# Group normalisation with 4 MB tiles and one group per partition, in place of 2 MB tiles and a cross-partition step, with a rewritten loop

## The chip, the cores and the metric

The kernel runs on one core of a Trainium2 chip. The metric is the device time of one execution in microseconds (us), median over several executions. The span in a profile runs from the first to the last instruction of the profiled execution and is here 1 to 2 us shorter than the metric. All runs quoted were classed as fast.

The engines are called by these names in the profile: PE is the matmul engine, PEld its weight loads, DVE is VectorE, ACT is ScalarE, POOL is GpSimd, and SPq is the queue from which the loads and stores are issued. L156 means line 156 of the kernel of that profile, so one function has different line numbers before and after. SBUF is the memory on the chip in which the tiles lie, in 128 partitions; PSUM is the memory into which the matmuls write.

## The reference

```python
# x: 128 samples x 1024 channels x 32 x 16, bf16; 32 groups of 32 channels
xr = x.reshape(B, G, C // G, H, W)
mu = xr.mean(axis=(2, 3, 4), keepdims=True)
var = ((xr - mu) ** 2).mean(axis=(2, 3, 4), keepdims=True)
xn = (xr - mu) / jnp.sqrt(var + 1e-5)
return xn.reshape(B, C, H, W) * g[None, :, None, None] + b[None, :, None, None]
```

A group has 32 x 512 = 16384 elements. The whole input is 134.2 MB, and the output is as large, so 268.4 MB have to be moved.

## The kernel before

A tile holds two samples in 128 partitions: 16 channels (16 KB) per partition, two partitions to a group, 2 MB in all, 64 tiles, eleven buffers. A matmul with a matrix of ones for partitions of the same group sums a tile over both partitions; VectorE reduces the resulting 512 columns to the mean. ScalarE takes the squares, and one quarter of the sum for the mean. A second small matmul joins the squares of the two partitions. Then come root, reciprocal, scale and bias, 16 scalings on VectorE (one per channel), and the store.

```python
# M: sums of a tile on PE (12 of 16 chunks; ScalarE's M1 sums the other 4)
nc.tensor.matmul(out=ps[:], lhsT=ind_b[:], rhs=xt[:, k*MMN:(k+1)*MMN], ...)
# R: columns -> -mean, on VectorE
nc.vector.tensor_scalar(out=jd[:], in0=st["ps"][:], ..., accum_out=negmean[:])
# Q: squares on ScalarE          # Gm: across partitions, on PE     # T: root on ScalarE
# A: reciprocal, scl, bia, then 16 scalings in place, on VectorE    # S: store
...
for s in range(-1, NT + 2):          # (bounds checks cut)
    M1(s + 1); M(s + 1)
    Gm(s - 1)
    A(s - 2)
    R(s + 1)
    Q(s)
    T(s - 1)
    S(s - 2); L(s - 2 + PREFETCH)
```

The order in which instructions are emitted is kept on each engine, for all that go through the kernel's helper `chain`. The scalings of step `s` belong to tile `s - 2`, the squares to tile `s`, the mean to tile `s + 1`. So the squares of a tile use a mean whose reduction was given to VectorE one step earlier, and ScalarE does not have to wait for it.

## Time and profile before

| | before |
|---|---|
| time, median | 639.52 us (639.23 to 639.78, 4 runs) |
| ScalarE busy | 590.7 us, 93% of the span |
| VectorE busy | 421.0 us, 66% |
| DMA | 430 GB/s in mid run, main queue 98.7% of the span |

Slices of the page of the kernel before: the span is cut into 40 equal pieces; a digit is the busy share in tenths, 9 meaning 90% or more.

```profile
ACT  1999999999999999999999999999999999999920
DMA  8999999999999999999999999999999999999993
GB/s 357 427 427 426 428 425 429 434 428 423 434 429 429 430 431 432 430 431 430 432 429 431 432 431 431 428 431 433 431 429 430 432 432 430 429 432 431 430 423 163
```

ScalarE and DMA are both full from the second slice to nearly the last. The digits can't tell them apart; the busy times in stretches of 100 us can (busy us and instructions of each engine, then clock, DMA share and GB/s):

```profile
200.00:300.00 100.00, 57.33 (x151) 21.84 (x154) 71.61 (x229) 99.64 (x53) 0.00 (x0) 0.68 1.01 431
500.00:600.00 100.00, 49.32 (x138) 20.42 (x140) 68.87 (x220) 97.11 (x51) 0.00 (x0) 0.68 1.01 430
```

In the order PE, PEld, DVE, ACT, POOL: ScalarE is busy 99.64 of 100 us early on and 97.11 late. It is ahead at first on prefetched tiles and slows in the last stretch, when loads come at DMA's pace: between 500 and 600 us it waits for loads for 2.6 us and PE for 48.9, between 200 and 300 us neither does. One pass of the loop in the timeline (start us, duration, engine, line, instruction; in brackets how long the engine was idle before and who released it):

```profile
301.19 0.24 ACT L221 ACTIVATE rstd<-ps_1567,eps_t 128x1 f32<-128x1 f32 x1
301.33 1.90 ACT L137 ACTIVATE ja<-xt 128x2048 bf16<-128x2048 bf16 x1
301.46 0.16 DVE L232 RECIPROCAL rstd<-rstd 128x1 f32<-128x1 f32 x1 [2.62 <-ACT rstd L221]
...
302.21 5.26 DVE L255 TENSOR_SCALAR xt<-xt,scl,bia 128x512 bf16<-128x512 bf16 x16
...
303.36 7.12 ACT L189 ACTIVATE ja<-xt,negmean 128x8192 bf16<-128x8192 bf16 x1
...
307.38 0.75 DVE L171 TENSOR_SCALAR_CACHE_REDUCE jd<-ps,ps_1616 128x512 bf16<-128x512 f32 x1
...
310.48 0.24 ACT L221 ACTIVATE rstd<-ps_1616,eps_t 128x1 f32<-128x1 f32 x1
```

The root repeats after 310.48 - 301.19 = 9.29 us, and the bracket on ScalarE's rows is absent: ScalarE does not wait in this pass. VectorE does its 16 scalings beside it and then waits 2.62 us, at no cost. A 2 MB tile in and out takes DMA 4.19 MB / 430 GB/s = 9.75 us, so the two limits are 5% apart, and DMA, the slower, sets the time in the long run.

### The profile page before, as it was taken

To read this page: it belongs to the slowest core of one execution; us is meant where nothing else is said; L and a number is where in the kernel's file an instruction comes from. 1 tells how busy PE (TensorE), PEld (TensorE's weight loads), DVE (VectorE), ACT (ScalarE), POOL (GpSimd) and SP (SyncE) were. 2 spreads that over 40 slices of the span, in tenths; PEclk is the share of its full clock that TensorE was granted. 3 is DMA by queue.
4 is the path that set the end of the run, shared out by engine and by line. 5 is a ranking of instruction groups with operands and counts; after the bars stand their busy time and mean duration, and the time that the engine had idled before them with its cause. 6 is when DMAs were issued, how large, how long until landed. Compare 5 with 4: busy or idle time off the path is not lost.

```text
span 637.8 us, 3899 instructions
## 1 busy us (share of the span) xinstructions
PE 326.3 (51%) x887; PEld 127.1 (20%) x904; DVE 421.0 (66%) x1349; ACT 590.7 (93%) x318; POOL 1.6 (0%) x6
## 2 busy tenths in 40 slices
PE   4654564556456555645654664464553654635300
PEld 1221122122112212211221222121221221212100
DVE  0086677668667766866776686677667667767680
ACT  1999999999999999999999999999999999999920
POOL 1000000000000000000000000000000000000000
PEclk9767767776776676666667667766766667666655
DMA  8999999999999999999999999999999999999993
GB/s 357 427 427 426 428 425 429 434 428 423 434 429 429 430 431 432 430 431 430 432 429 431 432 431 431 428 431 433 431 429 430 432 432 430 429 432 431 430 423 163
DMA packets 18774, 268.69 MB, mean 421 GB/s; under 512 B 2368, under 2 KB 2368, under 8 KB 2368
## 3 DMA queue, kind: packets, MB, share of 16 engines
q1 hardware_dynamic: 18752, 268.45, 98.7%
q8 instruction: 7, 0.11, 0.1%
q14 instruction: 15, 0.12, 0.0%
HBM read 134.23 MB, written 134.22 MB: 421 GB/s over the span
## 4 chain that ended last, share of the span: by engine, by line
ACT 53%; DMA 23%; issue 17%; DVE 2%; PE 1%; SPq 0%; DVEq 0%; ACTq 0%
ACT ja L189 38%; DMA out_dram<-xt 18%; ACT ja L137 14%; DMA xt<-in_x_dram 5%; DVE xt L255 2%; ACT rstd L221 1%; PE ps L154 1%; SPq L121 0%; DVE jd L171 0%; DVE bia L243 0%; DVE scl L237 0%; DVEq L330 0%; DVE rstd L232 0%; ACTq L137 0%
## 5 line engine op out<-in xcount | busy, mean ns | idle before, releaser
L189 ACT ACTIVATE ja<-xt,negmean 128x8192 bf16<-128x8192 bf16 x64 | 455.8, 7122 | 15.2 <-DVE jd L171 13.2
L154 PE MATMUL ps<-xt,ind_b 128*128 128x512 bf16 x759 | 301.9, 576 | 80.3 <-DMA xt<-in_x_dram 73.1
L255 DVE TENSOR_SCALAR xt<-xt,scl,bia 128x512 bf16<-128x512 bf16 x1024 | 336.6, 408 | 2.6 <-DVE bia L243 0.2
L154 PEld LDWEIGHTS <-ind_b 128*128 128x128 bf16 x776 | 108.6, 146 | 244.8 <-issue 162.4
L232 DVE RECIPROCAL rstd<-rstd 128x1 f32<-128x1 f32 x64 | 10.5, 164 | 169.1 <-ACT rstd L221 169.1
L137 ACT ACTIVATE ja<-xt 128x2048 bf16<-128x2048 bf16 x62 | 117.7, 1898 | 2.6 <-DMA xt<-in_x_dram 2.6
L243 DVE SCALAR_TENSOR_TENSOR bia<-scl,negmean,bet 128x16 f32<-128x16 f32 x64 | 15.0, 235 | 2.3
L237 DVE TENSOR_SCALAR scl<-gam,rstd 128x16 f32<-128x16 f32 x64 | 15.0, 234 | 2.2
L189 ACT ACTIVATION_READ_ACCUMULATOR ja<-xt,negmean 128x1 f32 x64 | 11.9, 186 | 0.0
L137 ACT ACTIVATION_READ_ACCUMULATOR ja<-xt 128x1 f32 x62 | 11.7, 189 | 0.0
L171 DVE TENSOR_SCALAR_CACHE_REDUCE jd<-ps 128x512 bf16<-128x512 f32 x2 | 1.4, 692 | 7.9 <-PE ps L154 7.9
L171 DVE TENSOR_SCALAR_CACHE_REDUCE jd<-ps,ps_170 128x512 bf16<-128x512 f32 x1 | 0.8, 755 | 6.6 <-PE ps_170 L206 6.6
L284 DVE CAST gam<-gam_b 128x16 f32<-128x16 bf16 x1 | 0.2, 174 | 6.4 <-DMA gam_b<-in_g_dram 6.4
L206 PE MATMUL ps_3186<-carry,ind_f 128*128 128x1 f32 x2 | 0.6, 362 | 6.7 <-ACT ja L189 6.7
L206 PE MATMUL ps_2155<-carry,ind_f 128*128 128x2 f32 x2 | 0.6, 362 | 4.8 <-ACT ja L137 4.8
L206 PE MATMUL ps_930<-carry,ind_f 128*128 128x2 f32 x2 | 0.6, 364 | 4.8 <-ACT ja L137 4.8
L206 PE MATMUL ps_1812<-carry,ind_f 128*128 128x2 f32 x2 | 0.6, 364 | 4.7 <-ACT ja L137 4.7
L206 PE MATMUL ps_587<-carry,ind_f 128*128 128x2 f32 x2 | 0.6, 364 | 4.7 <-ACT ja L137 4.7
L206 PE MATMUL ps_1469<-carry,ind_f 128*128 128x2 f32 x2 | 0.6, 362 | 4.6 <-ACT ja L137 4.6
L206 PE MATMUL ps_244<-carry,ind_f 128*128 128x2 f32 x2 | 0.6, 364 | 4.6 <-ACT ja L137 4.6
L206 PE MATMUL ps_1126<-carry,ind_f 128*128 128x2 f32 x2 | 0.6, 364 | 4.6 <-ACT ja L137 4.6
L206 PE MATMUL ps_2008<-carry,ind_f 128*128 128x2 f32 x2 | 0.6, 362 | 4.6 <-ACT ja L137 4.6
(319 smaller groups left out, 126.9 us busy)
## 6 DMA issues: line engine op xcount, KB each, us to landing
xt<-in_x_dram SPq DMA_DIRECT2D x64, 2048.0 KB, 24.2
out_dram<-xt SPq DMA_DIRECT2D x64, 2048.0 KB, 28.7
gam_b<-in_g_dram SPq DMA_DIRECT2D x2, 2.0 KB, 7.1
bet_b<-in_b_dram SPq DMA_DIRECT2D x2, 2.0 KB, 6.7
```

Of the source, the lines that this page charges most:

```text
L137: nc.scalar.activation(out=ja[:, 0 : na * MMN], in_=xt[:, (NMM - na) * MMN :], func=ACT.Identity, scale=-inv_n, accum_out=carry[:, 1:2],),
L154: nc.tensor.matmul(out=ps[:], lhsT=ind_b[:], rhs=xt[:, k * MMN : (k + 1) * MMN], start=(k == 0), stop=(k == npe - 1),),
L171: nc.vector.tensor_scalar(out=jd[:], in0=st["ps"][:], scalar1=-inv_n, scalar2=seed, op0=ALU.mult, op1=ALU.add, accum_out=negmean[:],),
L189: nc.scalar.activation(out=ja[:], in_=st["xt"][:], func=ACT.Square, bias=st["negmean"][:], scale=1.0, accum_out=carry[:, 0:1],),
L206: nc.tensor.matmul(out=ps2[:, 0:ncol], lhsT=ind_f[:], rhs=st["carry"][:, 0:ncol], start=True, stop=True,),
L221: nc.scalar.activation(out=rstd[:], in_=st["ps2"][:, 0:1], func=ACT.Sqrt, bias=eps_t[:], scale=inv_n),
L232: chain("dve", nc.vector.reciprocal(out=rstd[:], in_=rstd[:]))
L237: nc.vector.tensor_scalar(out=scl[:], in0=gam[:], scalar1=rstd[:], scalar2=None, op0=ALU.mult),
L243: nc.vector.scalar_tensor_tensor(out=bia[:], in0=scl[:], scalar=negmean[:], in1=bet[:], op0=ALU.mult, op1=ALU.add,),
L255: nc.vector.tensor_scalar(out=xt[:, k * HW : (k + 1) * HW], in0=xt[:, k * HW : (k + 1) * HW], scalar1=scl[:, k : k + 1], scalar2=bia[:, k ...
L284: nc.vector.tensor_copy(out=gam[:], in_=gam_b[:])
```

## The change

The intent: a tile of four samples with one whole group (32 channels, 32 KB) in each partition. Nothing has to be joined across partitions any more; the matmul matrix becomes the identity, ScalarE drops its share of the mean, and DMA rows are twice as long. The kernel keeps six such tiles in SBUF. The loop is rewritten, too. Core of the diff:

```diff
-NSAMP = 2
-XBUFS = 11
-PREFETCH = 9
-ACT_CHUNKS = 4
+XBUFS = 6
+UPFRONT = 6
+AHEAD = 5
+SQ_FREE = 4096
+A_HEAD = 12
...
-    x_v = x.rearrange("(t n) (cb k) h w -> t (n cb) (k h w)", n=NS, cb=CB)
+    x_v = x.rearrange("(t n) (g k) h w -> t (n g) (k h w)", n=NS, g=G)
...          # M: 32 matmuls with lhsT=eye[:]; Q: four squares of 4096 each
+    def V(i):   # variance: sum of 4 on VectorE, root on ScalarE,
+                # reciprocal, scl, bia on VectorE
...
-    for s in range(-1, NT + 2):
-        ...     # M1 M(s+1), Gm(s-1), A(s-2), R(s+1), Q(s), T(s-1), S(s-2), L
+    M(0)
+    R(0)
+    for i in range(NT):
+        Q(i)
+        V(i)
+        if i + 1 < NT:
+            M(i + 1)
+        A(i, 0, A_HEAD)
+        if i + 1 < NT:
+            R(i + 1)
+        A(i, A_HEAD, KC)
+        S(i)
+        j = i + AHEAD
+        if UPFRONT <= j < NT:
+            L(j)
```

The loads of gamma and beta also move from the queue of the tile loads to ScalarE's queue, in eight pieces instead of four.

More of the change, by code (lines that the diff above doesn't have):

```diff
@@ L37 @@
     HW = H * W
-    NS = NSAMP
-    assert B0 % NS == 0 and P % NS == 0
+    assert P % G == 0 and C % G == 0
+    NS = P // G
+    assert B0 % NS == 0
     NT = B0 // NS
-    CB = P // NS
-    assert C % CB == 0
-    KC = C // CB
+    KC = C // G
     F = KC * HW
-    cpg = C // G
-    assert cpg % KC == 0
-    PPG = cpg // KC
-    assert CB % PPG == 0
-    NELEM = cpg * HW
-    inv_n = 1.0 / float(NELEM)
+    inv_n = 1.0 / float(F)
     MMN = MM_FREE
-    assert F % MMN == 0
     NMM = F // MMN
-    assert 0 <= ACT_CHUNKS < NMM
-    x_v = x.rearrange("(t n) (cb k) h w -> t (n cb) (k h w)", n=NS, cb=CB)
-    o_v = out.rearrange("(t n) (cb k) h w -> t (n cb) (k h w)", n=NS, cb=CB)
-    g_v = g.rearrange("(cb k) -> cb k", cb=CB)
-    b_v = b.rearrange("(cb k) -> cb k", cb=CB)
+    NSQ = F // SQ_FREE
+    assert F % MMN == 0 and F % SQ_FREE == 0
+    x_v = x.rearrange("(t n) (g k) h w -> t (n g) (k h w)", n=NS, g=G)
+    o_v = out.rearrange("(t n) (g k) h w -> t (n g) (k h w)", n=NS, g=G)
+    g_v = g.rearrange("(g k) -> g k", g=G)
+    b_v = b.rearrange("(g k) -> g k", g=G)
     consts = ctx.enter_context(tc.tile_pool(name="consts", bufs=1))
@@ L63 @@
     jpool = ctx.enter_context(tc.tile_pool(name="jpool", bufs=1))
-    spool = ctx.enter_context(tc.tile_pool(name="spool", bufs=6))
+    spool = ctx.enter_context(tc.tile_pool(name="spool", bufs=4))
     pspool = ctx.enter_context(
         tc.tile_pool(name="pspool", bufs=3, space=bass.MemoryType.PSUM)
-    )
-    ps2pool = ctx.enter_context(
-        tc.tile_pool(name="ps2pool", bufs=3, space=bass.MemoryType.PSUM)
     )
@@ L82, in chain, with L @@
         return inst
-    ones_f = consts.tile([P, P], F32)
-    nc.vector.memset(ones_f[:], 1.0)
-    ind_f = consts.tile([P, P], F32)
-    nc.gpsimd.affine_select(
-        out=ind_f[:].rearrange("p (a c) -> p a c", c=PPG),
-        in_=ones_f[:].rearrange("p (a c) -> p a c", c=PPG),
-        pattern=[[-PPG, P // PPG], [0, PPG]],
-        compare_op=ALU.is_ge,
-        fill=0.0,
-        base=0,
-        channel_multiplier=1,
-    )
-    nc.gpsimd.affine_select(
-        out=ind_f[:].rearrange("p (a c) -> p a c", c=PPG),
-        in_=ind_f[:].rearrange("p (a c) -> p a c", c=PPG),
-        pattern=[[PPG, P // PPG], [0, PPG]],
-        compare_op=ALU.is_ge,
-        fill=0.0,
-        base=PPG - 1,
-        channel_multiplier=-1,
-    )
-    ind_b = consts.tile([P, P], BF16)
-    nc.vector.tensor_copy(out=ind_b[:], in_=ind_f[:])
+    state = {}
+    def L(i):
+        xt = xpool.tile([P, F], BF16, name="xt")
+        chain("sp", nc.sync.dma_start(out=xt[:], in_=x_v[i]))
+        state[i] = {"xt": xt}
+    for i in range(min(UPFRONT, NT)):
+        L(i)
     eps_t = consts.tile([P, 1], F32)
@@ L114 @@
     bet_b = consts.tile([P, KC], BF16)
-    state = {}
-    def L(i):
-        st = state.setdefault(i, {})
-        xt = xpool.tile([P, F], BF16, name="xt")
-        chain("sp", nc.sync.dma_start(out=xt[:], in_=x_v[i]))
-        st["xt"] = xt
-    def act_part(i):
-        return ACT_CHUNKS if i >= 2 else 0
-    def M1(i):
-        na = act_part(i)
-        if not na:
-            return
-        st = state[i]
-        xt = st["xt"]
-        carry = state[i - 2]["carry"]
-        ja = jpool.tile([P, F], BF16, name="ja")
-        chain(
-            "act",
-            nc.scalar.activation(
-                out=ja[:, 0 : na * MMN],
-                in_=xt[:, (NMM - na) * MMN :],
-                func=ACT.Identity,
-                scale=-inv_n,
-                accum_out=carry[:, 1:2],
-            ),
-        )
+    for n in range(NS):
+        chain("act", nc.scalar.dma_start(out=gam_b[n * G : (n + 1) * G, :], in_=g_v))
+        chain("act", nc.scalar.dma_start(out=bet_b[n * G : (n + 1) * G, :], in_=b_v))
+    ones_b = consts.tile([P, P], BF16)
+    nc.vector.memset(ones_b[:], 1.0)
+    eye = consts.tile([P, P], BF16)
+    nc.gpsimd.affine_select(
+        out=eye[:],
+        in_=ones_b[:],
+        pattern=[[-1, P]],
+        compare_op=ALU.is_equal,
+        fill=0.0,
+        base=0,
+        channel_multiplier=1,
+    )
+    gam = consts.tile([P, KC], F32)
+    bet = consts.tile([P, KC], F32)
+    nc.vector.tensor_copy(out=gam[:], in_=gam_b[:])
+    nc.vector.tensor_copy(out=bet[:], in_=bet_b[:])
     def M(i):
         st = state[i]
-        xt = st["xt"]
-        npe = NMM - act_part(i)
         ps = pspool.tile([P, MMN], F32, name="ps")
-        for k in range(npe):
+        for k in range(NMM):
             chain(
@@ L155, in M @@
                     out=ps[:],
-                    lhsT=ind_b[:],
-                    rhs=xt[:, k * MMN : (k + 1) * MMN],
+                    lhsT=eye[:],
+                    rhs=st["xt"][:, k * MMN : (k + 1) * MMN],
                     start=(k == 0),
-                    stop=(k == npe - 1),
+                    stop=(k == NMM - 1),
                 ),
@@ L167, in R @@
         jd = jpool.tile([P, MMN], BF16, name="jd")
-        seed = state[i - 2]["ps2"][:, 1:2] if act_part(i) else None
         chain(
@@ L174, in R @@
                 scalar1=-inv_n,
-                scalar2=seed,
+                scalar2=None,
                 op0=ALU.mult,
@@ L184, in Q @@
         st = state[i]
-        carry = spool.tile([P, 2], F32, name="carry")
-        ja = jpool.tile([P, F], BF16, name="ja")
-        chain(
-            "act",
-            nc.scalar.activation(
-                out=ja[:],
-                in_=st["xt"][:],
-                func=ACT.Square,
-                bias=st["negmean"][:],
-                scale=1.0,
-                accum_out=carry[:, 0:1],
-            ),
-        )
-        st["carry"] = carry
-    def Gm(i):
-        st = state[i]
-        ncol = 2 if (i + 2 < NT and act_part(i + 2)) else 1
-        ps2 = ps2pool.tile([P, 2], F32, name="ps2")
-        chain(
-            "pe",
-            nc.tensor.matmul(
-                out=ps2[:, 0:ncol],
-                lhsT=ind_f[:],
-                rhs=st["carry"][:, 0:ncol],
-                start=True,
-                stop=True,
-            ),
-        )
-        st["ps2"] = ps2
-    def T(i):
-        st = state[i]
+        sq = spool.tile([P, NSQ], F32, name="sq")
+        for k in range(NSQ):
+            ja = jpool.tile([P, SQ_FREE], BF16, name="ja")
+            chain(
+                "act",
+                nc.scalar.activation(
+                    out=ja[:],
+                    in_=st["xt"][:, k * SQ_FREE : (k + 1) * SQ_FREE],
+                    func=ACT.Square,
+                    bias=st["negmean"][:],
+                    scale=1.0,
+                    accum_out=sq[:, k : k + 1],
+                ),
+            )
+        st["sq"] = sq
+    def V(i):
+        st = state[i]
+        var = spool.tile([P, 1], F32, name="var")
+        jv = spool.tile([P, NSQ], F32, name="jv")
+        chain(
+            "dve",
+            nc.vector.tensor_scalar(
+                out=jv[:],
+                in0=st["sq"][:],
+                scalar1=inv_n,
+                scalar2=None,
+                op0=ALU.mult,
+                op1=ALU.add,
+                accum_out=var[:],
+            ),
+        )
         rstd = spool.tile([P, 1], F32, name="rstd")
@@ L221, in T @@
             nc.scalar.activation(
-                out=rstd[:], in_=st["ps2"][:, 0:1], func=ACT.Sqrt, bias=eps_t[:], scale=inv_n
+                out=rstd[:], in_=var[:], func=ACT.Sqrt, bias=eps_t[:], scale=1.0
             ),
         )
-        st["rstd"] = rstd
-    def A(i):
-        st = state[i]
-        rstd = st["rstd"]
-        negmean = st["negmean"]
-        xt = st["xt"]
         chain("dve", nc.vector.reciprocal(out=rstd[:], in_=rstd[:]))
@@ L245, in A @@
                 in0=scl[:],
-                scalar=negmean[:],
+                scalar=st["negmean"][:],
                 in1=bet[:],
@@ L251, in A @@
         )
-        for k in range(KC):
+        st["scl"], st["bia"] = scl, bia
+    def A(i, lo, hi):
+        st = state[i]
+        xt = st["xt"]
+        for k in range(lo, hi):
             chain(
@@ L257, in A @@
                     in0=xt[:, k * HW : (k + 1) * HW],
-                    scalar1=scl[:, k : k + 1],
-                    scalar2=bia[:, k : k + 1],
+                    scalar1=st["scl"][:, k : k + 1],
+                    scalar2=st["bia"][:, k : k + 1],
                     op0=ALU.mult,
@@ L265, in S @@
     def S(i):
-        st = state[i]
-        chain("sp", nc.sync.dma_start(out=o_v[i], in_=st["xt"][:]))
-        state.pop(i - 3, None)
-    for i in range(min(PREFETCH, NT)):
-        L(i)
-        if i == 0:
-            for n in range(NS):
-                chain(
-                    "sp",
-                    nc.sync.dma_start(out=gam_b[n * CB : (n + 1) * CB, :], in_=g_v),
-                )
-                chain(
-                    "sp",
-                    nc.sync.dma_start(out=bet_b[n * CB : (n + 1) * CB, :], in_=b_v),
-                )
-    gam = consts.tile([P, KC], F32)
-    bet = consts.tile([P, KC], F32)
-    nc.vector.tensor_copy(out=gam[:], in_=gam_b[:])
-    nc.vector.tensor_copy(out=bet[:], in_=bet_b[:])
-    for s in range(-1, NT + 2):
-        if 0 <= s + 1 < NT:
-            M1(s + 1)
-            M(s + 1)
-        if 0 <= s - 1 < NT:
-            Gm(s - 1)
-        if 0 <= s - 2 < NT:
-            A(s - 2)
-        if 0 <= s + 1 < NT:
-            R(s + 1)
-        if 0 <= s < NT:
-            Q(s)
-        if 0 <= s - 1 < NT:
-            T(s - 1)
-        if 0 <= s - 2 < NT:
-            S(s - 2)
-            if s - 2 + PREFETCH < NT:
-                L(s - 2 + PREFETCH)
+        chain("sp", nc.sync.dma_start(out=o_v[i], in_=state[i]["xt"][:]))
+        state.pop(i)
+    M(0)
[13 more added lines that the diff above has]
+            L(j)
 _INS = ['x', 'g', 'b']
```

## The prediction

> **What bounds the kernel now.** Two limits lie almost on each other. The slice rows show DMA at 9 tenths in nearly every slice and about 430 GB/s; one 2 MB tile in and out is 4.19 MB, so 9.75 us at that rate. The timeline shows ScalarE nearly as tight: its squares repeat every 9.29 us (7.12 us square, 1.90 us partial mean, their accumulator reads), and the stretches view shows it 99.6% busy from 100 to 500 us. The chain of waits is DMA from 450 us on. The software pipeline is two tiles deep, so no engine waits for the statistics of its own tile.
>
> **What changes.** Per 4 MB tile (32 of them):
> - DMA: the same bytes, 8.39 MB, 19.5 us at 430 GB/s. The queue is 98.7% busy with 16 KB rows already, so longer rows can save little.
> - PE: 32 identity matmuls, 0.43 us apart as in the timeline: 13.7 us. Not critical.
> - ScalarE: the mean share goes (1.9 us per 2 MB), the square becomes four pieces of 4096. [...] Its total falls from 591 to about 490 us.
> - DVE: 32 scalings at 0.329 us spacing (16 took 5.26 us), 10.5 us, plus about 2 us small work.
>
> **The critical path.** The engines' totals all fit under 19.5 us, but the two-tile pipeline is gone. In the new order, square(i+1) on ScalarE waits for the mean reduction (i+1), which on DVE stands behind the first 12 scalings of tile i; these need the root of tile i, which needs the end of square(i). So ScalarE and DVE form one serial loop per tile:
> - squares 15.3
> - variance sum on DVE about 0.3, root 0.24, with hand-overs about 0.1
> - reciprocal, scale, bias 0.75
> - 12 scalings 3.95
> - mean reduction 0.74
>
> Sum about 21.4 us, of which ScalarE idles about 6. That is above DMA's 19.5, so DMA starves in part: about 392 GB/s.
>
> **Ends.** Tile 0 is 4 MB and lands at about 13 us (2 MB landed at 8.6); its 32 matmuls take 9.5 us as the first 32 do now; first square at about 24. The gamma and beta loads now compete with six tile loads, and their casts stand before the first mean reduction on DVE; that may delay the start. Then 31 loops, 663 us, to 687. Last tile: 15.3 + 1.4 + 32 scalings 10.5 = 27, then its store alone, about 12: 726 us. Plus 1.6 us (time over span now) and 2 to 3 for the start: 731 us, that is 14% slower.
>
> **What would show it right.** ScalarE squares of consecutive tiles start about 21.4 us apart; before each first piece about 6 us idle, released by DVE's mean reduction; ScalarE busy near 67%; chain of waits mostly ScalarE squares and DVE scalings, little DMA; DMA about 390 GB/s with gaps; matmuls done well before they are needed.
>
> **What would make it wrong.** If the mean reduction (i+1) is not behind the 12 scalings on the path, the loop falls to DMA's 19.5 us and the time to about 640 to 650. If loads wait on stores in the one queue (a load needs the store of an earlier tile done), the loop grows past 21.4. A slow landing of gamma adds up to 15 us once.

The working of the squares' term rested on a figure that no trace of this case shows. The term that came out, 15.3 us a tile (about 490 us for 32), stands in the sums as the estimate; with it the loop came to 21.4 us and the time to 731 us. From the trace of the kernel before alone the estimate would be 15.1 us: 8192 elements took 7.12 us and 2048 took 1.90 us, which puts 4096 on a straight line at 3.64 us, and the next instruction started 0.13 us after the end (301.33 + 1.90 to 303.36). The loop would then be 21.2 us and the time about 725 us. The 12 us for the last store alone and the 15 us for a late gamma name no trace and are estimates, too; a store of the kernel after took 12.1 us to land (median), and the late casts gained 9.57 us at the start.

## The result, and the profile after

| | before | after |
|---|---|---|
| time, median | 639.52 us | 732.67 us (732.50 to 732.78, 4 runs) |
| span of the profiled run | 637.8 us | 731.1 us |
| ScalarE busy | 590.7 us (93%) | 497.5 us (68%) |
| VectorE busy | 421.0 us (66%) | 379.8 us (52%) |
| PE busy | 326.3 us (51%) | 288.9 us (40%) |

The ratio is 1.1459 (95% interval 1.1443 to 1.1475). Such a ratio is the mean time of one kernel's fast runs over that of the other's of the same rounds, so it is not quite the ratio of the medians. The new kernel is 14.6% slower, though every compute engine is busy for less time.

The slices of the page of the kernel after:

```profile
ACT  0267876666787666678766667876666787666670
DMA  9998599999999999999999999999999999934555
GB/s 377 431 437 364 229 385 390 403 402 377 397 404 402 373 402 401 402 375 402 402 374 402 402 402 372 403 402 402 373 420 385 378 400 398 401 145 202 229 229 229
```

ScalarE is no longer full. The DMA digits still read 9, which is a trap: the row below shows only about 395 GB/s. A 9 means "90% or more". In stretches:

```profile
200.00:300.00 100.00, 40.53 (x141) 15.85 (x142) 56.45 (x185) 74.11 (x43) 0.00 (x0) 0.69 0.96 397
300.00:400.00 100.00, 40.78 (x149) 15.94 (x146) 58.69 (x194) 71.16 (x42) 0.00 (x0) 0.72 0.96 396
```

No compute engine is full. DMA's share of 0.96 (1.01 before) is no proof of a full DMA either, because the share counts the time that packets take: the packet records of the kept traces show 1.27 us on average for a packet of 32 KB between 250 and 450 us here, against 1.22 us in the copy with 4 MB tiles further down, which moved 432 GB/s. When no engine is full, the time goes by in turns. One pass in the timeline of the kernel after shows who takes turns:

```profile
372.14 0.68 DVE L137 TENSOR_SCALAR_CACHE_REDUCE jd<-ps 128x512 bf16<-128x512 f32 x1
...
372.91 3.71 ACT L156 ACTIVATE ja<-xt,negmean 128x4096 bf16<-128x4096 bf16 x1 [5.45 <-DVE jd L137]
...
381.21 8.56 PE L121 MATMUL ps<-xt,eye 128*128 128x512 bf16 x32 [12.89 <-DMA xt<-in_x_dram]
...
388.24 0.16 DVE L173 TENSOR_SCALAR_CACHE_REDUCE jv<-sq 128x4 f32<-128x4 f32 x1 [8.96 <-ACT ja L156]
...
388.44 0.29 ACT L186 ACTIVATE rstd<-var,eps_t 128x1 f32<-128x1 f32 x1 [0.23 <-DVE jv L173]
388.77 0.17 DVE L190 RECIPROCAL rstd<-rstd 128x1 f32<-128x1 f32 x1 [0.36 <-ACT rstd L186]
...
389.53 3.97 DVE L218 TENSOR_SCALAR xt<-xt,scl,bia 128x512 bf16<-128x512 bf16 x12
393.42 0.68 DVE L137 TENSOR_SCALAR_CACHE_REDUCE jd<-ps 128x512 bf16<-128x512 f32 x1
...
394.19 3.71 ACT L156 ACTIVATE ja<-xt,negmean 128x4096 bf16<-128x4096 bf16 x1 [5.45 <-DVE jd L137]
```

Read it as a relay. The squares of a tile begin at 372.91 and end near 388.2 (15.3 us). VectorE, idle for 8.96 us, sums the variance; the root, the reciprocal, scale and bias follow until 389.53 (1.3 us). Twelve scalings take until 393.42 (3.9 us), and only then comes the mean of the next tile, for which ScalarE has waited; its squares begin at 394.19 (0.77 us later). The loop is 394.19 - 372.91 = 21.28 us, and 31 of them are 660 us. DMA's 8.39 MB would take 19.5 us at 430 GB/s.

The chain that ended last says the same (share of the span by engine; "issue" is time for which the profile shows no cause), before and then after:

```profile
ACT 53%; DMA 23%; issue 17%; DVE 2%; PE 1%; SPq 0%; DVEq 0%; ACTq 0%
```

```profile
ACT 68%; DVE 25%; DMA 4%; issue 1%; ACTq 0%; DVEq 0%
```

DMA goes from 23% of the chain to 4%, and VectorE from 2% to 25%. The list of waits of the kernel after (waiting line, releaser, us in total, times, longest) needs care:

```profile
PE ps L121 <- DMA xt<-in_x_dram: 343.9, 30, 18.5
...
DVE jv L173 <- ACT ja L156: 293.1, 32, 15.4
ACT ja L156 <- DVE jd L137: 199.1, 32, 30.1
```

The longest wait in total is PE's for loads. It would be easy to conclude that loads are late and six buffers are too few. PE is simply ahead: with three PSUM buffers it can run up to three tiles in front of VectorE, and then it has nothing to do until the next load lands. The waits that matter are the pair below it, ScalarE for VectorE and VectorE for ScalarE. The experiments test this reading.

### The profile page after: what moved, and what is told of

It is laid out like the page before. It is cut to its first block, busy times and chain, and to the rows that moved or that the text cites. A ratio compares the mean times of both kernels' runs of the same rounds, so it can differ in the third digit from the quotient of the medians.

```text
span 731.1 us, 3814 instructions
## 1 busy us (share of the span) xinstructions
PE 288.9 (40%) x1024; PEld 113.1 (15%) x1024; DVE 379.8 (52%) x1252; ACT 497.5 (68%) x290; POOL 0.5 (0%) x5
## 4 chain that ended last, share of the span: by engine, by line
ACT 68%; DVE 25%; DMA 4%; issue 1%; ACTq 0%; DVEq 0%
ACT ja L156 67%; DVE xt L218 18%; DVE jd L137 3%; DMA bet_b<-in_b_dram 3%; DMA xt<-in_x_dram 2%; ACT rstd L186 1%; DVE bia L201 1%; DVE scl L195 1%; DVE jv L173 1%; DVE rstd L190 1%; ACTq L156 0%; DVEq L272 0%; DVE bet L113 0%
## 5 line engine op out<-in xcount | busy, mean ns | idle before, releaser
L156 ACT ACTIVATE ja<-xt,negmean 128x4096 bf16<-128x4096 bf16 x128 | 474.7, 3708 | 202.2 <-DVE jd L137 199.1
L121 PE MATMUL ps<-xt,eye 128*128 128x512 bf16 x1024 | 288.9, 453 | 356.7 <-DMA xt<-in_x_dram 343.9
L121 PEld LDWEIGHTS <-eye 128*128 128x128 bf16 x1024 | 113.1, 113 | 532.0 <-DMA xt<-in_x_dram 343.4
L173 DVE TENSOR_SCALAR_CACHE_REDUCE jv<-sq 128x4 f32<-128x4 f32 x32 | 5.0, 157 | 293.1 <-ACT ja L156 293.1
L156 ACT ACTIVATION_READ_ACCUMULATOR ja<-xt,negmean 128x1 f32 x128 | 23.9, 187 | 0.0
L137 DVE TENSOR_SCALAR_CACHE_REDUCE jd<-ps 128x512 bf16<-128x512 f32 x32 | 21.8, 680 | 0.0
L186 ACT ACTIVATE rstd<-var,eps_t 128x1 f32<-128x1 f32 x32 | 9.4, 294 | 7.4 <-DVE jv L173 7.4
L190 DVE RECIPROCAL rstd<-rstd 128x1 f32<-128x1 f32 x32 | 5.3, 164 | 11.6 <-ACT rstd L186 11.6
L201 DVE SCALAR_TENSOR_TENSOR bia<-scl,negmean,bet 128x32 f32<-128x32 f32 x32 | 8.0, 251 | 1.1
L195 DVE TENSOR_SCALAR scl<-gam,rstd 128x32 f32<-128x32 f32 x32 | 7.7, 242 | 1.1
## 6 DMA issues: line engine op xcount, KB each, us to landing
out_dram<-xt SPq DMA_DIRECT2D x32, 4096.0 KB, 12.1
gam_b<-in_g_dram ACTq DMA_DIRECT2D x4, 2.0 KB, 15.7
bet_b<-in_b_dram ACTq DMA_DIRECT2D x4, 2.0 KB, 17.1
```

The lines of the kernel that those rows point to most:

```text
L121: nc.tensor.matmul(out=ps[:], lhsT=eye[:], rhs=st["xt"][:, k * MMN : (k + 1) * MMN], start=(k == 0), stop=(k == NMM - 1),),
L137: nc.vector.tensor_scalar(out=jd[:], in0=st["ps"][:], scalar1=-inv_n, scalar2=None, op0=ALU.mult, op1=ALU.add, accum_out=negmean[:],),
L156: nc.scalar.activation(out=ja[:], in_=st["xt"][:, k * SQ_FREE : (k + 1) * SQ_FREE], func=ACT.Square, bias=st["negmean"][:], scale=1.0, acc ...
L173: nc.vector.tensor_scalar(out=jv[:], in0=st["sq"][:], scalar1=inv_n, scalar2=None, op0=ALU.mult, op1=ALU.add, accum_out=var[:],),
L186: nc.scalar.activation(out=rstd[:], in_=var[:], func=ACT.Sqrt, bias=eps_t[:], scale=1.0),
L190: chain("dve", nc.vector.reciprocal(out=rstd[:], in_=rstd[:]))
```

## The experiments

The theory is the serial loop of the prediction: squares, variance, 12 scalings, mean of the next tile. Rival A says that the new DMA geometry (4 MB tiles, 32 KB rows, six buffers) is slower in itself, 395 GB/s in place of 430. Rival B says that late loads hold PE and so everything. All edits are against the new kernel unless something else is said, and every result was correct except for the two copies. The kernel before was timed beside each set of runs, at 639.2 to 639.6 us.

### How long the mean waits: 20, 6 and 0 scalings in front of it

```diff
-A_HEAD = 12
+A_HEAD = 20      # h20;  6 in h6;  0 in h0
```

> The mean reduction of the next tile is moved behind 20 scalings instead of 12. Serial-loop theory: the loop grows by 8 scalings at 0.3275 us, 2.62 us, from 21.28 to 23.90 us, 31 times: 732.7 + 81 = 814 us; the squares of consecutive tiles start 23.9 us apart. Rival A (DMA with 4 MB tiles, 32 KB rows and six buffers is slower): total work, bytes and rows are the same, so at most a few us change, about 733 to 740 us. Rival B (PE waits on late loads): likewise about 733 us.

> The mean reduction of the next tile stands behind 6 scalings instead of 12. Serial-loop theory: loop 21.28 - 6 x 0.3275 = 19.3 us, just under DMA's 19.5; the sum of start 32.4, 31 loops, last tile 27, last store 12 and 1.6 gives 672 us. As DMA has no slack left at this pace, up to 680 is possible. Rival A or B (the place of the reduction matters only as a switch, not by its length): 645 or 733 us.

> The mean reduction of the next tile is moved in front of all 32 scalings. Serial-loop theory: the loop falls by 12 scalings to about 17.3 us, under DMA's 19.5 us for 8.39 MB, so the kernel becomes DMA bound: about 645 us, 636 to 660, DMA near 430 GB/s, and ScalarE then waits on something other than the 12 scalings. Rival A (the new DMA geometry gives only 395 GB/s): stays at 725 to 735 us. Rival B (late loads hold PE): stays at about 730 us.

| scalings in front of the mean | time, median | ratio to before |
|---|---|---|
| 20 (h20) | 812.85 us | 1.2715 |
| 12 (the change) | 732.67 us | 1.1459 |
| 6 (h6) | 672.56 us | 1.0521 |
| 0 (h0) | 644.66 us | 1.0085 (1.0068 to 1.0101) |

From 20 to 12 the time falls by 80.2 us for 8 scalings, and from 12 to 6 by 60.1 us for 6: both 10.02 us for each scaling moved (the sums expected were 814 and 672 us), which is 31 loops of 0.323 us, the spacing of the scalings. No work was removed. From 6 to 0 the same slope would give another 60 us, but only 27.9 us come: another limit takes over.

The loops in the traces show the same slope. The first squares of consecutive tiles start 23.87 us apart in h20, 21.28 in the change, 19.34 in h6 and, at about 100 us, where loads are plentiful, 17.28 in h0. ScalarE's wait for the mean goes with them, 8.04, 5.45, 3.51 and 1.46 us; one line each of h20, h6 and h0:

```profile
342.59 3.71 ACT L156 ACTIVATE ja<-xt,negmean 128x4096 bf16<-128x4096 bf16 x1 [8.04 <-DVE jd L137]
...
322.48 3.71 ACT L156 ACTIVATE ja<-xt,negmean 128x4096 bf16<-128x4096 bf16 x1 [3.51 <-DVE jd L137]
...
118.85 3.71 ACT L156 ACTIVATE ja<-xt,negmean 128x4096 bf16<-128x4096 bf16 x1 [1.46 <-DVE jd L137]
```

The limit that takes over in h0 can be seen in its waits:

```profile
PE ps L121 <- DMA xt<-in_x_dram: 306.7, 31, 24.2
...
DVE jd L137 <- PE ps L121: 31.0, 14, 3.0
```

The mean reduction, which never waited in the kernel after, now waits for PE's sums 14 times, and PE for loads: DMA has caught up with the loop. The slices of h0 confirm it, at 424 to 441 GB/s but for one hole (231, then 392) and the two ends:

```profile
GB/s 367 441 431 424 231 424 392 439 434 428 429 437 426 424 441 434 425 429 438 426 425 436 440 424 432 435 429 430 438 433 427 429 437 434 426 436 430 436 349 269
```

So a one-number edit of the order, with the tile size untouched, gives back 88.0 of the 93.2 us that the change cost. Rivals A and B expected about 733 us for h20 and 725 to 735 for h0; both fail.

### The mean of the next tile in front of the variance as well

```diff
         Q(i)
-        V(i)
         if i + 1 < NT:
             M(i + 1)
-        A(i, 0, A_HEAD)
-        if i + 1 < NT:
             R(i + 1)
-        A(i, A_HEAD, KC)
+        V(i)
+        A(i, 0, KC)
```

> The mean reduction of the next tile stands before the variance work of the present one, so ScalarE's squares wait for nothing on VectorE but the variance sum and their own root: ScalarE's loop would be about 15.9 us, against 17.3 in the run with the reduction in front of all scalings. Serial-loop theory with a DMA floor: both are under DMA's 19.5 us, so no gain over that run: 640 to 650 us. If ScalarE and VectorE still set the pace there, this run is about 31 times 1.4 us faster, near 600 us.

Measured 643.08 us (642.59 to 643.40), ratio 1.0060. In the part of the trace where loads are plentiful, the first squares of two consecutive tiles start 15.7 us apart (158.24 and 173.96 us), as expected, against 21.28. The total gains only 1.6 us over h0, and the intervals of the two ratios overlap. With the relay broken up, ScalarE's pace stops mattering, and DMA sets the time: it is 66% of this run's chain, against 4% before the edit.

### Four buffers instead of six

```diff
-XBUFS = 6
-UPFRONT = 6
-AHEAD = 5
+XBUFS = 4
+UPFRONT = 4
+AHEAD = 3
```

> Four tile buffers instead of six, loads three tiles ahead instead of five; the schedule is untouched. Serial-loop theory: loads land 21.9 us after issue and three loops are 64 us, so nothing changes once running: 733 us, at most 740. Rival B (PE's 344 us of waits on loads hold the kernel, too few buffers): clearly slower, over 755 us, and squares further apart than 21.28 us.

Measured 732.70 us, against 732.67 with six. In the waits of this run PE waits even longer for loads, and the pair that matters is unchanged to 0.1 us:

```profile
PE ps L121 <- DMA xt<-in_x_dram: 400.5, 31, 49.7
...
DVE jv L173 <- ACT ja L156: 293.0, 32, 15.4
ACT ja L156 <- DVE jd L137: 199.0, 32, 30.0
```

57 us more of PE waiting cost nothing. (Much of the difference is one wait of 49.7 us early on, against 18.5 us in the kernel after: with four buffers fewer loads can run ahead of the first stores.) Rival B falls.

### Loads and stores alone, in the new and the old geometry

```diff
-        ...            # all of M, R, Q, V, A (and in the old kernel M1, Gm, T)
     for i in range(NT):
         S(i)
         ...            # next load as before
```

> Wrong result on purpose: the new kernel's loads and stores, 4 MB tiles with 32 KB rows and six buffers, with all arithmetic taken out; the output is x. Serial-loop theory: the new geometry moves bytes as fast as the old, 268.4 MB at about 430 GB/s plus about 5 us of ends: 628 to 635 us. Rival A (the new geometry gives only 395 GB/s): 675 us or more.

> Wrong result on purpose: the old kernel's loads and stores, 2 MB tiles with 16 KB rows and eleven buffers, without arithmetic. Both theories: 628 to 638 us, since the old kernel at 639 us keeps DMA busy 98.7% of its span. Serial-loop theory: within 1% of the copy with 4 MB tiles; rival A: over 5% faster than it.

Measured 633.57 us for 4 MB tiles (633.16 to 633.96) and 632.15 us for 2 MB tiles (632.08 to 632.75). The new geometry is as fast as the old to 0.2%, and longer rows save nothing. Rival A falls. These two are also the floor for loads and stores in these two orders: the kernel before is about 1% above it (the ratios of the copies to it are 0.9914 and 0.9891), so with them no arrangement of the arithmetic could have gained much more than that. Another order of loads and stores was not tried.

### The start: gamma and beta

In the kernel after, the first mean stands behind the casts of gamma and beta in VectorE's order. Its timeline:

```profile
13.25 0.32 ACTq L96 DMA_DIRECT2D bet_b<-in_b_dram  x1
13.27 16.85 PE L121 MATMUL ps<-xt,eye 128*128 128x512 bf16 x64 [13.27 <-DMA xt<-in_x_dram]
28.04 0.18 DVE L112 CAST gam<-gam_b 128x32 f32<-128x32 bf16 x1 [26.94 <-DMA gam_b<-in_g_dram]
31.60 0.18 DVE L113 CAST bet<-bet_b 128x32 f32<-128x32 bf16 x1 [3.38 <-DMA bet_b<-in_b_dram]
31.69 0.68 DVE L137 TENSOR_SCALAR_CACHE_REDUCE jd<-ps 128x512 bf16<-128x512 f32 x1
...
32.42 3.71 ACT L156 ACTIVATE ja<-xt,negmean 128x4096 bf16<-128x4096 bf16 x1 [30.12 <-DVE jd L137]
```

Tile 0 landed at 13.2 us, but the first square starts at 32.42: the last small load is issued at 13.25 us and lands near 31.6. The packet records of the kept trace show how. Between 4.8 and 31.1 us ScalarE's queue moved 384 packets of 64 bytes or less, and in the same time the tile loads started 351 packets of 32 KB, of mostly 1.21 us each: about one small packet for each large one. If each of the 16 DMA engines carries 24 of the small packets, each behind a large one, that is an estimate of 24 x 1.21 = 29 us, near the 26 us of the trace; no run tests whether they do. The copy with 4 MB tiles, without arithmetic, shows the same 384 and 351. From issue to landing the small loads took 15.7 us (gamma) and 17.1 us (beta, both medians) beside six 4 MB loads, against 7.1 and 6.7 us in the kernel before, where they stood in the same queue behind the first 2 MB load.

The first attempt moved the casts in the text of the kernel only:

```diff
-    nc.vector.tensor_copy(out=gam[:], in_=gam_b[:])
-    nc.vector.tensor_copy(out=bet[:], in_=bet_b[:])
...
     M(0)
     R(0)
+    nc.vector.tensor_copy(out=gam[:], in_=gam_b[:])      # cast_late; in cast_late2
+    nc.vector.tensor_copy(out=bet[:], in_=bet_b[:])      # each in chain("dve", ...)
```

> The two casts of gamma and beta are moved behind the first mean reduction on VectorE; nothing else. My reading: the first square waited until 32.4 us because beta landed at 31.6; the first tile's matmuls were done near 23 us, so the first square starts at about 24 us and the whole loop shifts by 8.5 us: about 724 us, loop still 21.28 us. Rival: if the loads upfront or DMA set the pace from there, the start is given back and the time stays at 732 us.

It measured 732.87 us, and the expectation was missed. The trace says why: the casts still ran at 28.00 and 31.57 us, in front of the first mean at 31.66. They were not in the chain that fixes VectorE's order, and the scheduler placed them as before. The run tested nothing. With the casts tied in:

> The same edit as the run before, but now tied into VectorE's order, because in that run the trace showed the casts still in front of the first mean reduction (the scheduler had put them back), so it tested nothing. My reading: first square at about 24 us instead of 32.4, loop still 21.28 us, 724 us. Rival (DMA or the loads set the pace from the start): the shift is given back, 732 us.

Measured 723.04 us, 9.6 us less. The first square now starts 9.57 us earlier, by its timeline:

```profile
22.85 3.71 ACT L154 ACTIVATE ja<-xt,negmean 128x4096 bf16<-128x4096 bf16 x1 [20.56 <-DVE jd L135]
...
27.76 0.18 DVE L232 CAST gam<-gam_b 128x32 f32<-128x32 bf16 x1 [4.94 <-DMA gam_b<-in_g_dram]
```

In this serial loop the start that moved was carried to the end in full.

### A version that beats the change and, narrowly, the kernel before

h0 loses time in a hole and at its end. Both show in its stretches (same columns as before):

```profile
70.00:75.00 5.00, 5.00 (x23) 2.14 (x22) 5.00 (x17) 4.94 (x5) 0.00 (x0) 0.90 0.04 15
```

After the six loads at the start and the first store, DMA has nothing to do until the second store is issued (77 us); 15 GB/s in this stretch. At the end, DMA moved 33 to 115 GB/s from 625 to 631 us and then the last 4 MB alone. The first edit stores the last tile in quarters (h0tail), the second adds the late casts (best1), and the last takes the late casts without the quarters (h0cast).

```diff
-A_HEAD = 12                                   # all three
+A_HEAD = 0
...
+        else:                                 # h0tail and best1: the last tile
+            for k in range(0, KC, 8):
+                A(i, k, k + 8)
+                chain("sp", nc.sync.dma_start(out=o_v[i][:, k*HW:(k+8)*HW], in_=...))
...
+    chain("dve", nc.vector.tensor_copy(...))  # best1 and h0cast: casts behind R(0)
```

> The reduction in front of all scalings (the run at 644.7 us), and the last tile is stored in four quarters, each after its 8 scalings, instead of once after 32. In the run at 644.7 us DMA lay nearly idle from 625 to 630 us and then moved the last 4 MB alone for 12 us. Expected: the last quarter needs about 4.5 us after the last scaling, so 7 us less: 637.5 us, 635 to 640.

> The run before with the two casts behind the first mean reduction as well (tied into VectorE's order). The first store is issued 9.5 us earlier, so that the hole in DMA's work at 64 to 80 us (231 GB/s in that slice) nearly closes: 6 to 7 us less, about 631 us, 628 to 635; that would be 1% under the old kernel and level with the copies without arithmetic (632.2 and 633.6). If the hole stays, 637 us.

> The reduction in front of all scalings and the late casts, but the last tile stored in one piece: it divides the gain of the 637.0 us run between its two edits. The quarters alone gave nothing (645.2 against 644.7), because the DMA's last few us, at 25 to 75 GB/s, came behind them instead of in the gap before the last store. If the late casts gave all of it by closing the hole at 64 to 80 us: 637 us, 635 to 638.5. If the quarters help once the hole is closed: 640 us or more.

| | time, median | ratio to before |
|---|---|---|
| h0 | 644.66 us | 1.0085 |
| h0tail | 645.15 us | 1.0091 (1.0075 to 1.0106) |
| best1 | 637.03 us | 0.9968 (0.9956 to 0.9981) |
| h0cast | 636.82 us (636.12 to 637.16) | 0.9957 (0.9943 to 0.9970) |

The late casts gain 7.8 us: the first two stores are issued from 51.6 us on in h0cast, 60.0 in h0, and the hole closes (349 GB/s or more in every 5 us from 60 to 80 us). The quarters gain nothing, alone or with the late casts, and both expectations that counted on them were missed. (For best1, 637 us was expected if the hole stayed. The time is the one named, but the hole did close; what was missing is the gain of the quarters.) The stretches at the end of h0tail:

```profile
631.00:633.00 2.00, 0.00 (x0) 0.00 (x0) 0.46 (x2) 0.00 (x0) 0.00 (x0) 0.50 0.97 406
633.00:635.00 2.00, 0.00 (x0) 0.00 (x0) 0.00 (x0) 0.00 (x0) 0.00 (x0) 0.50 1.03 430
635.00:637.00 2.00, 0.00 (x0) 0.00 (x0) 0.00 (x0) 0.00 (x0) 0.00 (x0) 0.50 0.32 135
637.00:639.00 2.00, 0.00 (x0) 0.00 (x0) 0.00 (x0) 0.00 (x0) 0.00 (x0) 0.50 0.17 74
639.00:641.00 2.00, 0.00 (x0) 0.00 (x0) 0.00 (x0) 0.00 (x0) 0.00 (x0) 0.50 0.06 25
```

DMA stays full until 635 us and then takes another 6 us or so for a remnant at 25 to 135 GB/s. The same thin end stands in the kernel before (33 GB/s from 630 to 634 us) and in the copies, which have no arithmetic (66 GB/s from 625 to 628 us with 4 MB tiles). In h0 a thin stretch lies in the gap in front of the last store; with the quarters it comes after everything else. That the gap hid it fits all these traces, but it was only argued. At 430 GB/s all 16 DMA engines together move 27 GB/s each, so 33 GB/s is by this estimate what one or two of them move: some engines seem to finish later than the rest.

The packet records of the kept trace agree with this for the copy with 4 MB tiles. Its 8192 packets of 32 KB can be put into 16 rows, in which each packet starts as the one before it ends, with about 512 packets to a row; the records name no engine, but a row looks like the work of one. Thirteen rows end between 623.0 and 624.8 us and three at 628.4, 628.4 and 630.6. The three had no more packets than the rest, and their last packets took the usual 1.21 us; but some 20 to 28 packets of each, spread over the run, took over 1.25 us, and only 2 to 7 in each of the others. If a row is one engine's work, three of the 16 fell behind during this run, and showed it at the end. Which engines, and why, stays open.

h0cast is 0.43% faster than the kernel before, which is clear of noise, and takes 13% less time than the change as made. It is 0.5% above the copy with 4 MB tiles.

## Why the prediction was right

- **The time.** Predicted 731 us, measured 732.67. That the two agree within 2 us is in part luck, as the last point shows.
- **The loop.** Predicted 21.4 us, measured 21.28. The parts: squares 15.3 predicted, 15.3 measured; variance sum, root, reciprocal, scale, bias and hand-overs about 1.4 against 1.29; 12 scalings 3.95 against 3.89; mean 0.74 against 0.77. The scalings were a little too dear because 16 in 5.26 us contains the last one in full (0.41 us); the spacing is 0.323 us, not 0.329. The root took 0.29 us and not 0.24 (0.294 and 0.242 us in the traces). Its input is now in SBUF; before it was in PSUM. No run tests whether that is the cause.
- **ScalarE's squares.** The 15.3 us a tile were the estimate; measured were 3.708 us a piece, 3.83 us start to start and 15.3 us for the four.
- **No gain from longer rows.** Shown by the copies, within 0.2% (632.15 us with 16 KB rows, 633.57 with 32 KB).
- **PE is not critical.** Shown by b4, in which PE waits 57 us longer at the same time. Its cost was over-estimated: 13.7 us a tile, where the pass shown took 8.56 us and the page has 288.9 us for 32 tiles. As PE was not on the path, that cost the prediction nothing.
- **DMA starves at about 390 GB/s.** 393 to 397 GB/s in the stretches from 100 to 600 us.
- **What would make it wrong.** "If the mean reduction (i+1) is not behind the 12 scalings on the path [...] the time to about 640 to 650": h0 is that case, at 644.66 us.
- **The term that was mis-sized** is the start. It said "first square at about 24" and "2 to 3 for the start" for gamma and beta. The first square started at 32.4 us, and taking the casts out of its way moved it by 9.57 us. The rest of the sum was a few us too large (31 loops of 0.12 us less are 3.7 us), which is why the total came within 2 us: two errors of opposite sign. The prediction had named this risk ("a slow landing of gamma"), but not sized it right.

The new kernel did what it promised for each engine: ScalarE's work fell by 93 us, and the cross-partition matmuls went. It gave up the two-tile distance between squares and scalings to do so. In the old order up to 99.6% of ScalarE's time was work (100 to 500 us). In the new order ScalarE stands idle for 27% of each loop (21.28 us less 15.3 of squares and 0.29 of root), most of it the wait of 5.45 us created by where one instruction stands in VectorE's order. No run keeps the old two-tile distance with 4 MB tiles; what that would give is not shown.

## What to carry to other kernels

When engines hand a tile back and forth, add up one lap of the relay before adding up each engine's work: here all engine totals lay under DMA's 19.5 us a tile, and the lap was 21.3 us. An instruction that releases another engine belongs in front of independent work in its queue; moving one reduction past 12 scalings was worth 88 us without changing any work. The longest entry in a list of waits may belong to an engine that is only ahead: take buffers away, and see whether the time moves (here PE's waits for loads went from 343.9 to 400.5 us, and the time from 732.67 to 732.70).
